# Linear attention and a gated long convolution on one core: the first batch's gate ahead of its convolution, a filter transform from half sums, v staged in pieces

## The chip, the cores and the metric

The kernel runs on 1 core of one Trainium2 chip. The metric is device time in microseconds of one execution. The engines are TensorE (PE: matmuls, with its weight loads shown as PEld), VectorE (DVE), ScalarE (ACT), GpSimd (POOL) and SyncE (SP); transfers are issued from the queues of POOL (inputs) and SP (outputs).

## The reference, cut to what matters

```python
# q, k, v: (8, 8, 576, 64); w_proj: (512, 1536); filter_fft: (576, 512); w_out: (512, 512)
def _attn_ref(q, k, v):
    theta = pi / 2 * arange(S) / S
    phi = lambda x: concat([relu(x) * cos(theta), relu(x) * sin(theta)], -1)   # 64 -> 128
    kv = einsum('bhsf,bhsd->bhfd', phi(k), v)
    z = sum(phi(k), axis=2)
    return einsum('bhsf,bhfd->bhsd', phi(q), kv) / (einsum('bhsf,bhf->bhs', phi(q), z) + 1e-6)

def reference(q, k, v, w_proj, filter_fft, w_out):
    x = heads side by side of _attn_ref(q, k, v)           # (8, 576, 512)
    x1, x2, x3 = split(x @ w_proj, 3)
    x2_conv = irfft(rfft(x2, axis=1) * rfft(filter_fft, axis=0), axis=1)
    return (x1 * x2_conv * x3) @ w_out
```

## The kernel before

The eight batches go one after another; all tiles of a batch fit on the chip. The names used below, for a batch b:

- `phi` (`emit_phi`): the features of q and k, 12 products each on DVE (recorded at line 90), from a raw tile that a POOL transfer fills. The raw tiles (q, k and v of all batches) share four buffers, so a load waits until an earlier raw tile was read to its end.
- `va` (`emit_va`, L114): ACT copies v of all 8 heads from its raw tile to `va`, next to a constant column.
- `qt` (L416): 48 transposes of q's features on PE, evicted by DVE (L422) and ACT (L426). `kv` (L403): 48 matmuls, evicted by ACT (L408). `num` (L440): 40 matmuls in four parts, and the division on DVE (L448), which gives `att`.
- `fx` (L463, L475): the first, fixed part of the transform over the sequence (`fm`), by four channel groups, evicted by ACT (L467, L479).
- `x2` (L498): the middle third of w_proj in three blocks of 8 matmuls of 512 columns, evicted by ACT (L503). `dft` (L512): two matmuls for each of three blocks, with the tables `tre` and `tim`, an eviction by ACT (L514) and four DVE products with the filter's transform (L517 to L522), which give `yf`.
- `gate` (L535): x1 and x3, the outer thirds of w_proj, 16 matmuls of 288 columns for each of four channel groups; ACT evicts x1 (L541) and DVE multiplies the two (L543) into `g`.
- `inv` (L561): 24 matmuls with the inverse tables `ire` and `iim`, an eviction by ACT (L565) and three DVE products (L566 to L568), the last with `g`. `out` (L584): 20 matmuls of 512 columns with w_out, evicted by ACT (L588) and stored from SP's queue.

Ahead of the loop stands a setup: the features, kv, num, fx and x2 of batch 0, the tables of the forward transform, the filter's transform (`emit_h_tables`, `emit_h`), the inverse tables (`emit_inv_tables`, whose range reduction runs on POOL, L238 and L241), and q, k and v of batch 1. The filter's transform multiplies all 576 rows of the filter (6 on each of 96 partitions) with cosines and sines: 36 matmuls of 512 columns and 6 for one extra frequency. The loop then runs, for b, dft, gate and inv of batch b, x2 of b, num and fx of b + 1, out of b - 1, and loads, features, qt and kv of b + 2. PSUM holds four units of two banks; every step above takes one or two.

Each engine executes its own instructions strictly in one order, POOL's transfers included. This order isn't the one of the calls: a scheduler lays it out when the program is built. It takes the calls' order as priority, and moves an instruction ahead where by its own reckoning of durations that one could start earlier. A wait that it reckoned shorter than it is on the chip holds up everything behind it on that engine.

The pool `late` (g, eo, y, os) takes the memory of the setup's tiles, so its first tile waits until the setup is through.

Of the kernel before, what the change touches and what calls it, by code (L numbers as in the profile page):

```python
# [17 lines left out]
def kernel(  # L18
# [320 lines left out]
    def emit_h_tables():  # L339
        frow, sj = cc["frow"], cc["sj"]  # L340
# [3 lines left out]
        hc = cc["hc"] = setupp.tile([NP, NJ, HS], FP16, tag="hc", name="hc")  # L344
        hs_ = cc["hs"] = setupp.tile([NP, NJ, HS], FP16, tag="hs_", name="hs_")
        for g in range(2):
            tn = setupp.tile([NP, NCOL], FP32, tag="tn_big", name=f"tn_h{g}")
            for jj in range(3):
                tsc(
                    tn[:, ds(jj * HS, HS)], frf, sj[0:NP, 3 * g + jj : 3 * g + jj + 1],  # L350
                    AL.mult, 1.0 / S, AL.mult,
                )
            trig(
                NP, tn,
                hs_[:, 3 * g : 3 * g + 3].rearrange("p a b -> p (a b)"),
                hc[:, 3 * g : 3 * g + 3].rearrange("p a b -> p (a b)"),
                NCOL,
            )
# [347 lines left out]
```

## Time and profile before

| | |
|---|---|
| runs | 305.18, 305.05, 301.96 us |
| median | 305.05 us |
| profiled execution | 306.0 us, of which the span from first to last instruction is 304.2 us |
| PE busy | 257.1 us, 85% of the span |
| DVE busy | 213.3 us, 70% |
| ACT busy | 199.8 us, 66% |
| POOL busy | 38.4 us, 13% |
| mean granted clock of PE | 0.948 |

All rows are of the profiled execution. Times in them are microseconds from the span's start, unless they are marked as ns. A busy share is the time that instructions of the engine were running; matmuls and weight loads overlap.

### The profile page before, as it was taken

The page shows a single profiled execution, that of the slowest core. Times are in us where ns is not written, and L with a number is a line of the kernel's source. Part 1 is how long each engine was busy: PE and PEld are TensorE (multiplying, and loading weights), DVE is VectorE, ACT ScalarE, POOL GpSimd, SP SyncE. Part 2 cuts the span into 40 slices and gives each one's busy share as a digit, 9 for nine tenths or more (in the row PEclk, how much of TensorE's full clock was granted, in tenths as well). Part 3 has the DMA queues.
Part 4 walks back from the last instruction along what each step waited for, and adds up shares of the span by engine and source line. Part 5 has one row for each costly group of instructions (what it writes and reads, how often), then busy time and mean ns, then how long its engine had stood idle before and what let it go on. Part 6 is the DMA issues. An engine that isn't in the chain of part 4 may idle for free.

```text
span 304.2 us, 6038 instructions
## 1 busy us (share of the span) xinstructions
PE 257.1 (85%) x2394; PEld 182.1 (60%) x2394; DVE 213.3 (70%) x684; ACT 199.8 (66%) x248; POOL 38.4 (13%) x43
## 2 busy tenths in 40 slices
PE   0647984589984599999999999999999999999970
PEld 0445541567862386768676866686678768757630
DVE  4999980487997285898589759966876558607900
ACT  2358672975750877977797778777487748757532
POOL 8330890110140300030012000000000000000000
PEclk9999998558999599999999999999999999999997
DMA  7999919924145590597149414003200410050055
GB/s 101 210 206 202 181 13 198 164 27 69 13 70 78 76 158 18 141 129 105 41 117 174 62 44 115 1 1 86 74 0 2 131 27 2 0 155 3 0 156 155
DMA packets 26828, 26.66 MB, mean 88 GB/s; under 512 B 1616, under 2 KB 22096, under 8 KB 26800
## 3 DMA queue, kind: packets, MB, share of 16 engines
q0 software_dynamic: 21040, 16.84, 37.0%
q1 hardware_dynamic: 5760, 9.44, 11.3%
q8 instruction: 18, 0.29, 0.4%
q14 instruction: 10, 0.08, 0.1%
HBM read 33.69 MB, written 9.44 MB: 142 GB/s over the span
## 4 chain that ended last, share of the span: by engine, by line
PE 59%; DVE 17%; DMA 9%; ACT 5%; POOL 3%; issue 3%; SPq 1%; ACTq 0%; POOLq 0%; DVEq 0%
PE x L535 21%; PE out L584 9%; PE inv L561 7%; DMA vraw<-in_v_dram 7%; PE x L498 6%; PE qt L416 6%; DVE kp L90 5%; PE fx L463 4%; POOL tg_a L238 3%; DVE qp L90 3%; DVE att L448 3%; PE dft L512 2%; ACT x2f L503 2%; DMA qraw<-in_q_dram 2%; PE kv L403 2%
## 5 line engine op out<-in xcount | busy, mean ns | idle before, releaser
L535 PE MATMUL x<-fx,wp 128*128 128x288 f16 x512 | 69.7, 292 | 0.0
L535 PEld LDWEIGHTS <-wp 128*128 128x128 f16 x512 | 51.1, 100 | 15.0 <-issue 1.0
L498 PE MATMUL x<-wp,fx 128*96 128x512 f16 x192 | 46.6, 391 | 2.8 <-ACT fx L479 1.5
L467 ACT CAST fx<-fx 128x960 f16<-128x960 f32 x32 | 30.3, 958 | 15.2 <-PE fx L463 15.2
L416 PE MATMUL qt<-perm,qp 96*128 96x96 f16 x384 | 23.6, 222 | 17.0 <-DVE qp L90 8.6
L584 PE MATMUL out<-wo,y 128*128 128x512 f16 x160 | 37.4, 379 | 0.0
L503 ACT ACTIVATE x2f<-x 96x1024 f16<-96x1024 f32 x24 | 24.1, 1017 | 18.2 <-PE x L498 18.2
L416 PEld LDWEIGHTS <-qp 96*128 96x128 f16 x384 | 21.1, 106 | 22.2 <-DVE qp L90 9.9
L498 PEld LDWEIGHTS <-fx 128*96 128x96 f16 x192 | 22.8, 127 | 18.9 <-DVE att L448 2.0
L543 DVE TENSOR_TENSOR g<-x,x1s 128x288 f16<-128x288 f32 x64 | 27.1, 444 | 8.1 <-PE x L535 8.1
L114 ACT COPY va<-vraw 96x3072 f16<-96x3072 f16 x8 | 22.0, 2754 | 16.0 <-DMA vraw<-in_v_dram 16.0
L588 ACT ACTIVATE os<-out 128x1024 f32<-128x1024 f32 (+1 forms) x24 | 20.7, 882 | 15.5 <-PE out L584 10.9
L517 DVE TENSOR_TENSOR m<-xf,ha 96x1024 f16<-96x1024 f16 x24 | 16.3, 679 | 19.9 <-ACT xf L514 19.8
L426 ACT COPY qpt<-qt 128x600 f16<-128x600 f16 x32 | 20.0, 661 | 13.9 <-DVE qpt L422 13.8
L448 DVE TENSOR_TENSOR att<-num,rcp 128x640 f16<-128x640 f32 x32 | 26.0, 819 | 0.2
L541 ACT CAST x1s<-x 128x576 f16<-128x576 f32 x32 | 20.5, 640 | 7.2 <-PE x L535 4.8
L422 DVE COPY qpt<-qt 128x600 f16<-128x600 f16 x32 | 14.7, 466 | 14.2 <-PE qt L416 13.8
L584 PEld LDWEIGHTS <-y 128*128 128x128 f16 x160 | 15.1, 98 | 15.3
L514 ACT CAST xf<-dft 96x1024 f16<-96x1024 f32 x24 | 23.5, 1009 | 0.8 <-PE dft L512 0.8
L561 PEld LDWEIGHTS <-yf 96*128 96x128 f16 x192 | 18.6, 98 | 4.4
L403 PE MATMUL kv<-va,kp 96*128 96x65 f16 x384 | 15.8, 206 | 5.5 <-ACT va L114 4.0
L463 PE MATMUL fx<-fm,att 128*128 128x240 f16 x128 | 19.6, 284 | 0.8 <-DVE att L448 0.8
(145 smaller groups left out, 396.7 us busy)
## 6 DMA issues: line engine op xcount, KB each, us to landing
qraw<-in_q_dram POOLq DMA_DIRECT2D x8, 576.0 KB, 6.2
kraw<-in_k_dram POOLq DMA_DIRECT2D x8, 576.0 KB, 7.8
vraw<-in_v_dram POOLq DMA_DIRECT2D x8, 576.0 KB, 8.5
out_dram<-os SPq DMA_DIRECT2D x24, 192.0 KB, 2.6
out_dram<-os SPq DMA_DIRECT2D x24, 128.0 KB, 2.4
wp<-in_moe_w_proj_dram POOLq DMA_DIRECT2D x3, 512.0 KB, 14.2
out_dram<-os SPq DMA_DIRECT2D x24, 64.0 KB, 2.0
filt<-in_moe_filter_fft_dram POOLq DMA_DIRECT2D x1, 576.0 KB, 10.4
```

The source lines that it names most:

```text
L90: nc.vector.tensor_scalar(out=out, in0=in0, scalar1=s1, scalar2=s2, op0=op0, op1=op1)
L416: nc.tensor.transpose(u[:, hh, ds(j * NP, NP)], qp[:, j, 2 * hp + hh].rearrange("p a b -> p (a b)"), perm,)
L448: nc.vector.tensor_tensor(out=att[:, :, ds(hp * 128, 128)].rearrange("p t (h d) -> p h t d", h=2), in0=nv[:, :, :, 0:D], in1=rcp.unsqueeze ...
L463: nc.tensor.matmul(u[:, t // 2, 0:480].rearrange("p (g o) -> p g o", o=20)[:, :, ds((t % 2) * 10, 10)], att[:, t, ds(c * 128, 128)], fm, s ...
L467: nc.scalar.copy(out=fx[:, c, :, 0:40].rearrange("p g (u o) -> p u g o", u=2), in_=u[:, :, 0:480].rearrange("p u (g o) -> p u g o", o=20),)
L498: nc.tensor.matmul(u[0:NP, comp], fx[:, c, ds(comp * 6 + 2 * bl, 2)].rearrange("p a b -> p (a b)"), wp16[:, c, ds(DM, DM)], start=(c == 0) ...
L503: nc.scalar.mul(out=x2f[:, bl], in_=u[0:NP], mul=X2SC)
L514: nc.scalar.copy(out=xf, in_=u[0:NP])
L535: nc.tensor.matmul(u[:, hf, 0:HS], wp16[:, i, ds(w * DM + c * 128, 128)], fx[:, i, ds(12 + 6 * hf, 6)].rearrange("p a b -> p (a b)"), star ...
L543: nc.vector.tensor_tensor(out=(g[:, c, 0:HS] if hf == 0 else g[:, c, HS:S][:, ::-1]).rearrange("p (j i o) -> p j i o", j=3, i=6), in0=us[1 ...
L561: nc.tensor.matmul(u[:, comp, 0:HS], yf[:, bl, comp, ds(c * 128, 128)], tab[:, bl], start=(bl == 0), stop=(bl == 2),)
L584: nc.tensor.matmul(u[:, x], y[:, c, ds(OT[t], 128)], wo16[:, c], start=(c == 0), stop=(c == NC - 1),)
```

## The change

Four things are changed.

- Order: in the setup, the gate of batch 0 goes behind its fx and ahead of the forward tables and x2. `g` moves from the pool `late` to the pool `work`, so that it doesn't wait for the setup's end. The rest of batch 0 (dft, inv) and num and fx of batch 1 are written into the setup as well, with loads, features, va, qt and kv of batch 2; the loop begins at batch 1.
- Loads: w_proj's outer thirds are first, the middle third next, then q and k of batch 1, the filter, v of batch 1 and w_out.
- Filter: it is loaded as two halves of 288 rows, 3 rows on each of 96 partitions. POOL makes the sum and the difference of the halves (`feo`, 96x1536 each). The blocks 1 and 2 of the transform take one of these each (3 matmuls instead of 6 for each part); block 0 takes both halves, the second one with tables (`hb`) multiplied by an alternating sign on DVE; the extra frequency takes 3 matmuls. The tables need one round instead of two. The tiles `ha` and `hi` become one tile `h3` (imaginary, real, real part), evicted in one instruction a block.
- `va` is copied in four pieces of two heads.

```diff
     def emit_va(b):
-        nc.scalar.copy(
-            out=va_buf[b % 2][:, :, :, 0:D],
-            in_=raw_t[(b, "v")].rearrange("p h (j d) -> p h j d", j=NJ),
-        )
+        for x in range(4):
+            hs = slice(2 * x, 2 * x + 2)
+            nc.scalar.copy(
+                out=va_buf[b % 2][:, hs, :, 0:D],
+                in_=raw_t[(b, "v")][:, hs].rearrange("p h (j d) -> p h j d", j=NJ),
+            )
...
     def load_filter():
-        nc.gpsimd.dma_start(out=filt16, in_=moe_filter_fft.rearrange("(p j) n -> p (j n)", j=NJ))
+        for x in range(2):
+            nc.gpsimd.dma_start(
+                out=filt16[:, x],
+                in_=moe_filter_fft[ds(x * HS, HS)].rearrange("(p j) n -> p (j n)", j=3),
+            )
...
-        hc = cc["hc"] = setupp.tile([NP, NJ, HS], FP16, tag="hc", name="hc")
-        hs_ = cc["hs"] = setupp.tile([NP, NJ, HS], FP16, tag="hs_", name="hs_")
-        for g in range(2):
-            tn = setupp.tile([NP, NCOL], FP32, tag="tn_big", name=f"tn_h{g}")
...
+        tn = setupp.tile([NP, NCOL], FP32, tag="tn_big", name="tn_h")
+        for j in range(3):
+            tsc(tn[:, ds(j * HS, HS)], frf, s3[0:NP, j : j + 1], AL.mult, 1.0 / S, AL.mult)
+        trig(NP, tn, hs_.rearrange("p a b -> p (a b)"), hc.rearrange("p a b -> p (a b)"), NCOL)
+
+        hb = cc["hb"] = setupp.tile([NP, 2, 3, NP], FP16, tag="hb", name="hb")
+        for x, tab in ((0, hs_), (1, hc)):
+            nc.vector.tensor_tensor(
+                out=hb[:, x], in0=tab[:, :, 0:NP],
+                in1=cc["sgn"].unsqueeze(1).to_broadcast([NP, 3, NP]), op=AL.mult,
+            )
...
     def emit_h():
+        for x, op in ((0, AL.add), (1, AL.subtract)):
+            nc.gpsimd.tensor_tensor(
+                out=feo[:, x].rearrange("p j n -> p (j n)"), in0=filt16[:, 0], in1=filt16[:, 1], op=op
+            )
         for bl in range(3):
             u = unit(f"h_ps{bl}")
-            for ci, tab in ((0, hc), (1, hs_)):
-                for j in range(NJ):
+            for ci, tab in ((0, hs_), (1, hc)):
+                if bl == 0:
+                    mm = [(tab[:, j, 0:NP], fa[:, 0, j]) for j in range(3)]
+                    mm += [(hb[:, ci, j], fa[:, 1, j]) for j in range(3)]
+                else:
+                    mm = [(tab[:, j, ds(bl * NP, NP)], feo[:, 2 - bl, j]) for j in range(3)]
+                for x, (l, r) in enumerate(mm):
                     nc.tensor.matmul(
-                        u[0:NP, ci], tab[:, j, ds(bl * NP, NP)], filt16[:, j],
-                        start=(j == 0), stop=(j == NJ - 1),
+                        u[0:NP, ci], l, r, start=(x == 0), stop=(x == len(mm) - 1)
                     )
-            nc.scalar.activation(out=ha[:, bl, 0], in_=u[0:NP, 0], func=AF.Copy, scale=sc)
-            nc.scalar.activation(out=hi[:, bl], in_=u[0:NP, 1], func=AF.Copy, scale=sc)
-            nc.vector.tensor_copy(out=ha[:, bl, 1], in_=ha[:, bl, 0])
+            nc.scalar.activation(out=h3[:, bl, 0:2], in_=u[0:NP], func=AF.Copy, scale=sc)
+            nc.vector.tensor_copy(out=h3[:, bl, 2], in_=h3[:, bl, 1])
...
     def emit_gate(b, c):
-            moe[b]["g"] = late["p"].tile([128, NC, S], FP16, tag="g", name=f"g{b}")
+            moe.setdefault(b, {})["g"] = work.tile([128, NC, S], FP16, tag="g", name=f"g{b}")
...
-    load_filter()
-    load_wp(1)
     load_wp(0)
     load_wp(2)
+    load_wp(1)
+    load_qk(1, "q")
+    load_qk(1, "k")
+    load_filter()
+    load_v(1)
+    load_wo()
     emit_cols()
     emit_pads()
+    emit_fm()
...
     emit_kv(0)
-    emit_fm()
     for hp in range(4):
         emit_num(0, hp)
     emit_fx(0)
+    emit_rows()
+    for c in range(NC):
+        emit_gate(0, c)
+    emit_fwd_tables()
     emit_x2(0)
-    emit_rows()
-    emit_fwd_tables()
-    emit_input_dma(1)
-    load_wo()
-    emit_h_tables()
-    emit_h()
-    emit_inv_tables()
     emit_phi(1, "q")
     for hp in range(4):
         emit_qt(1, hp)
+    emit_h_tables()
     emit_phi(1, "k")
     emit_va(1)
     emit_kv(1)
+    emit_h()
+    for hp in range(4):
+        emit_num(1, hp)
+    emit_dft(0)
+    emit_inv_tables()
+    emit_fx(1)
     setup_stack.close()
     late["p"] = ctx.enter_context(tc.tile_pool(name="late", bufs=1))
-
-    for b in range(0, B + 1):
+    for c in range(NC):
+        emit_inv(0, c)
+    emit_input_dma(2)
+    emit_phi(2, "q")
+    emit_phi(2, "k")
+    emit_va(2)
+    for hp in range(4):
+        emit_qt(2, hp)
+    emit_kv(2)
+
+    for b in range(1, B + 1):
```

## Rows read from the trace of the kernel before

**Rows 1.** The page's first part: busy us, share of the span, instructions, by engine.
```profile
PE 257.1 (85%) x2394; PEld 182.1 (60%) x2394; DVE 213.3 (70%) x684; ACT 199.8 (66%) x248; POOL 38.4 (13%) x43
```

**Rows 2.** Busy time by stretch; last columns granted clock, DMA share, GB/s.
```profile
30.70:82.60 51.90, 41.96 (x317) 28.64 (x318) 35.71 (x103) 34.47 (x41) 16.58 (x9) 0.80 0.64 95
48.00:56.80 8.80, 0.69 (x13) 0.58 (x13) 0.47 (x1) 3.74 (x4) 0.70 (x1) 0.66 1.31 203
56.80:65.50 8.70, 7.99 (x125) 7.82 (x125) 6.46 (x22) 6.75 (x9) 0.07 (x1) 0.50 0.56 76
94.70:102.00 7.30, 0.67 (x4) 0.28 (x3) 2.43 (x8) 3.75 (x3) 0.71 (x1) 0.77 0.12 17
133.70:163.40 29.70, 28.96 (x295) 20.94 (x295) 24.14 (x74) 23.11 (x29) 2.31 (x3) 1.00 0.60 105
```

**Rows 3.** The chain that ended last, at the holes: start, us, what.
```profile
31.68 9.09 POOL tg_a L238
...
43.66 9.38 DMA vraw<-in_v_dram
...
87.56 10.66 DMA vraw<-in_v_dram
98.25 2.75 ACT va L114
```

**Rows 4.** The waits: who waited for whom, total us, times, longest.
```profile
ACT va L114 <- DMA vraw<-in_v_dram: 16.0, 3, 7.5
```

**Rows 5.** The chain again, in the rhythm of the loop, PE's steps.
```profile
133.73 0.59 PE dft L512 x2
134.32 1.96 PE x L535 x16
...
144.13 2.94 PE inv L561 x24
147.07 1.73 PE out L584 x8
148.80 0.51 PE qt L416 x12
...
163.35 0.59 PE dft L512 x2
...
241.88 1.52 PE kv L403 x48
243.41 1.74 PE x L498 x8
245.15 0.62 PE num L440 x20
```

**Rows 6.** The timeline: start, us, engine, line, operation; idle before in brackets.
```profile
14.93 2.77 ACT L114 COPY va<-vraw 96x3072 f16<-96x3072 f16 x1
17.75 2.80 PE L403 MATMUL kv<-va,kp 96*128 96x65 f16 x48 [4.01 <-ACT va L114]
30.76 6.83 PE L498 MATMUL x<-wp,fx 128*96 128x512 f16 x24 [1.47 <-ACT fx L479]
33.23 2.75 ACT L114 COPY va<-vraw 96x3072 f16<-96x3072 f16 x1 [2.53 <-DMA vraw<-in_v_dram]
40.84 2.17 DVE L90 TENSOR_SCALAR qp<-qraw,ccol 96x512 f16<-96x512 f16 x1
40.85 2.00 POOL L241 TENSOR_TENSOR tg_a<-tg_a,tn_inv 96x864 f32<-96x864 f32 x1
```

**Rows 7.** Groups of instructions: line, engine, shape, count, busy us, mean ns.
```profile
L114 ACT COPY va<-vraw 96x3072 f16<-96x3072 f16 x8 | 22.0, 2754 | 16.0 <-DMA vraw<-in_v_dram 16.0
L248 ACT ACTIVATE tg_a<-tg_a 96x864 f32<-96x864 f32 x3 | 2.8, 920 | 0.1
...
L244 DVE SCALAR_TENSOR_TENSOR tg_a<-tg_a,tn_h 96x864 f32<-96x864 f32 x2 | 2.1, 1040 | 0.0
L224 DVE TENSOR_TENSOR fm<-coef,match 128x240 f16<-128x240 f32 x1 | 0.4, 391 | 0.0
```

More of the change, by code (lines that the diff above doesn't have):

```diff
@@ L343, in emit_h_tables @@
         nc.vector.memset(wr_col[0:1], 1.0 / S)
-        hc = cc["hc"] = setupp.tile([NP, NJ, HS], FP16, tag="hc", name="hc")
-        hs_ = cc["hs"] = setupp.tile([NP, NJ, HS], FP16, tag="hs_", name="hs_")
-        for g in range(2):
-            tn = setupp.tile([NP, NCOL], FP32, tag="tn_big", name=f"tn_h{g}")
[L348 to L357, printed above, removed]
-            )
+        s3 = small("s3", 3)
@@ new lines, in emit_h_tables @@
+        nc.vector.tensor_copy(out=s3, in_=cc["s3_i"])
+        hc = cc["hc"] = setupp.tile([NP, 3, HS], FP16, tag="hc", name="hc")
+        hs_ = cc["hs"] = setupp.tile([NP, 3, HS], FP16, tag="hs_", name="hs_")
+        tn = setupp.tile([NP, NCOL], FP32, tag="tn_big", name="tn_h")
+        for j in range(3):
+            tsc(tn[:, ds(j * HS, HS)], frf, s3[0:NP, j : j + 1], AL.mult, 1.0 / S, AL.mult)
+        trig(NP, tn, hs_.rearrange("p a b -> p (a b)"), hc.rearrange("p a b -> p (a b)"), NCOL)
@@ new lines, in emit_h_tables @@
+        hb = cc["hb"] = setupp.tile([NP, 2, 3, NP], FP16, tag="hb", name="hb")
[3 more added lines that the diff above has]
+                in1=cc["sgn"].unsqueeze(1).to_broadcast([NP, 3, NP]), op=AL.mult,
+            )
+        alt = cc["alt"] = setupp.tile([NP, 2], FP16, tag="alt", name="alt")
+        par = cc["par"]
+        tsc(alt[:, 0:1], par[0:NP], -2.0, AL.mult, 1.0, AL.add)
+        tsc(alt[:, 1:2], par[0:NP], 2.0, AL.mult, -1.0, AL.add)
@@ L376, in emit_h @@
-            nc.vector.tensor_copy(out=ha[:, bl, 1], in_=ha[:, bl, 0])
+            nc.scalar.activation(out=h3[:, bl, 0:2], in_=u[0:NP], func=AF.Copy, scale=sc)
+            nc.vector.tensor_copy(out=h3[:, bl, 2], in_=h3[:, bl, 1])
         u = unit("h_nyq")
-        for j in range(NJ):
+        for j in range(3):
             nc.tensor.matmul(
-                u[0:1, 0], alt[:, j : j + 1], filt16[:, j], start=(j == 0), stop=(j == NJ - 1)
+                u[0:1, 0], alt[:, j % 2 : j % 2 + 1], feo[:, 0, j], start=(j == 0), stop=(j == 2)
@@ L381, in emit_h @@
             )
-        nc.scalar.activation(out=ha[0:1, 0, 1], in_=u[0:1, 0], func=AF.Copy, scale=1.0 / S)
+        nc.scalar.activation(out=h3[0:1, 0, 2], in_=u[0:1, 0], func=AF.Copy, scale=1.0 / S)
     kp_t, qp_t, kvs_t, att_t, fx_t, xt_t = {}, {}, {}, {}, {}, {}
@@ L491, in emit_x2 @@
         if 0 in bls:
-            moe[b] = {"x2f": work.tile([NP, 3, 2, DM], FP16, tag="x2f", name=f"x2f{b}")}
+            moe.setdefault(b, {})["x2f"] = work.tile([NP, 3, 2, DM], FP16, tag="x2f", name=f"x2f{b}")
         x2f = moe[b]["x2f"]
```

21 lines of the change are left out of this document (10 added, 11 removed).

## The prediction, made before the result was known

> **What bounds the kernel now.** I read the page's first part, then the busy time by stretch, then the chain of waits, then the timeline around its holes. The first part [rows 1] has TensorE (PE) busy 85% of the span and no other engine above 70%. That average hides two different regimes. In the stretch table [rows 2] PE is busy nearly all the time while the loop is in its rhythm, but from 30.7 to 102 us there are two holes: 48.0 to 56.8 with 0.69 us of PE work, and 94.7 to 102.0 with 0.67. [...]
>
> The chain of waits names the cause of both holes [rows 3]: a load of v, 9.38 us in one and 10.66 us in the other, after which ScalarE (ACT) makes its copy of v into va. ACT takes its instructions in order, and the copy stands ahead of evictions whose inputs are long there: in the first hole those of the filter's transform, in the second those of x2. PE waits for these. The waits view puts the sum of three such waits at 16.0 us [rows 4]. Ahead of the first load stands 9.09 us of GpSimd (POOL) work for the inverse tables: the loads are issued from POOL's queue, so nothing is issued meanwhile.
>
> In the rhythm, PE is the bound. From one dft to the next takes 163.35 - 133.73 = 29.62 us [rows 5]. The same rows price the work at 2.4 GHz: x2 3 x 1.74 = 5.22; num 2 x 0.61 = 1.22; gate 4 x 1.96 = 7.84; inv 2.94; gate, fx and inv together 147.07 - 134.32 = 12.75, so fx 1.97; out 2.5 x 1.73 = 4.33; qt 4 x 0.51 = 2.04; kv 1.52. A matmul of 512 columns is 1.74 / 8 = 0.2175, so dft's six are 1.31. Sum 28.4; a cycle has 1.22 us beyond it.
>
> From 30.7 to 133.7 us, 103.0 us, PE does: batch 0 x2, dft, gate, inv, out 21.64; batch 1 all but out 24.07; batch 2 qt, kv, num, fx, x2 11.97; batch 3 qt, kv, num 4.78; the filter's 42 matmuls 9.1. That is 71.6, so 31.4 us are lost there. What lies behind 133.7 is untouched by the change but for va's pieces.
>
> **The change part by part.**
>
> *Order.* Batch 0's gate needs only fx and w_proj's outer thirds, which now load first; it moves to 30.7 us and fills PE while tables and filter are made. All its work comes along: 64 matmuls, 4 evictions, 8 products. By itself it saves nothing; it is cover, 7.84 us, for the holes. Batch 1's num and fx move ahead of batch 0's inverse too. In all PE has then, in the stretch of 103.0 us, 62.46 + 27 x 0.2175 = 68.3 us. I keep two losses: the slow start of PE's long work (the first x2 took 6.83 instead of 5.22 [rows 6], 1.6), which the gate will now pay, and 1.22 for each of some 2.3 cycles, 2.8. That gives 72.7, a gain of 30.3 with no hole left. This is the upper bound.
>
> *Filter transform.* 42 matmuls become 12 + 6 + 6 + 3 = 27: 3.3 us of PE, counted in the 68.3. One table round goes: three activations of about 0.92 [rows 7], 2.8 us of ACT; on VectorE (DVE) five instructions of which the largest is 1.04, so 2 to 3 us, against two products for hb at about 0.4 each (nearest row: the fm product, 0.39 [rows 7]) and two tiny ones. These hide under loads before 30.7; without that cover 1 us. Three evictions of two halves replace six of one half: the same columns. The filter comes in two transfers of the same bytes. Both at nothing: ACT stands idle beside them, and one more issue on POOL is under a microsecond.
>
> *Sum and difference on POOL.* This is new: two POOL instructions of 96x1536. The trace has two POOL rows to price them, both of 96x864 in f32 [rows 3, 6]: 2.00 us for the two-input form (2.3 ns an element) and 9.09 us for the one-input form (10.5 ns). So 7.1 us for both at the one end, 32.3 us at the other. I take the lower, since it is the same operation; but DVE ran back to back next to the 9.09 and this may be why, so I keep the upper. The other direction shows too: beside the 2.00 one DVE instruction, a product of 96x512, took 2.17 us [rows 6]. [...]
>
> *DVE in the filled stretch.* From 30.7 to the end of batch 0's inverse (82.6) DVE has 35.71 us of work now [rows 2]. PE's part of it after the change is x2, dft, gate, inv of batch 0 (17.31), qt, kv, num, fx of batch 1 (6.75), filter 5.9, slow start 1.6: 31.6 us. DVE's is then about 33, plus up to 7.1 of standing for POOL; six of it (phi of batch 2) can slip. From 0 to 9 us on the path; I take 5.
>
> *POOL's queue.* Behind these two and the inverse tables stand the loads of k and v of batch 2. Before, v of batch 2 was issued at 43.66 [rows 3]. The filter lands later than before: ten loads were issued before v of batch 1 was there, whose copy starts at 33.23 [rows 6], and the filter is now ninth, one load of 0.58 MB at 203 GB/s [rows 2] or 2.8 us earlier, so at about 30. If POOL then does 7.1 + 9.09 + 2.00, it is free at about 48.5, 5 us later than before, and v lands near 58. Batch 2's kv is due on PE near 64: in time. But an early va piece in ACT's queue can hold it as before.
>
> *va in four pieces.* An instruction of 864 elements takes 0.92 and one of 3072 takes 2.75 [rows 7]: 0.83 ns an element and 0.2 fixed, so four pieces cost some 0.3 us more a batch, less than the 6.6 us that ACT stands idle in a cycle (23.11 busy of 29.7 [rows 2]); if that cover went, 2.4 us over eight batches. A piece waits for the same single load, so splitting doesn't end a wait. It lets kv start after the first piece: batch 0's copy starts at 14.93 and kv at 17.75, for 2.80 us [rows 6]. Four pieces end near 18.0, the last quarter of kv is 0.7, so kv ends at 18.7 instead of 20.5. I take 1.5 of the 1.8, since att on DVE is behind it; from 0 to 1.8.
>
> *Waits on v.* Both holes with the half-clock stretch cost: 8.1 + 6.9 idle, and 56.8 to 65.5 took 8.7 for 4.3 us of work: 4.4. Together 19.4. The inverse tables stay on POOL and v's loads in its queue, so I don't count both as gone: I leave one of the second's size, 7.5. Bounds 0 and 19.4.
>
> Sum by the profiled execution: span 304.2 - 30.3 - 1.5 = 272.4, + 5 + 7.5 = 284.9. This execution took 306.0 by its own time and the median is 305.05; I add to the span what the median has over 304.2, 0.85: **286 us**.
>
> **The rivals.**
>
> *POOL becomes the bound.* At 10.5 ns an element the two new instructions take 32.3; from 30 with the tables' 11.1 ahead, the difference is there at 73.4. PE has until then gate, x2, qt, kv, num, fx (19.8) and 1.6 of slow start: done at 52.2. It waits 21 us, and some 3 follow at the lower clock, as behind the first hole: 272.4 + 24 = 296.4 by span, 297. For it: 9.09 us. Against it: the same form took 2.00. It decides from the point where the difference comes after 52. [...]
>
> *Both holes stay.* ACT's order puts va pieces ahead of urgent evictions again: 272.4 + 5 + 19.4 = 296.8, 298. For it: three waits of this kind now. Against: later cycles have none, and the cover is there.
>
> *No hole comes back:* 272.4 to 277, 273 to 278.
>
> *Slower.* A piece of batch 2's va stands in ACT's queue ahead of the filter's evictions, and v of batch 2 is issued only when POOL is through, at 73.4, landing 9.4 later at 82.8. Then va 3, evictions 3, num, dft, fx, inv and the products between them 9, lower clock 2: batch 0's inverse ends near 100 instead of 82.6, and without the second hole (7 + 1) the kernel is 9 us slower, 314. It decides from a landing after about 73. Against it: this needs POOL at its slowest and that order.
>
> **How the numbers follow.** Forecast 0.52 (its own range 279 to 293), no hole 0.12, POOL bound 0.14, both holes 0.12, slower mechanism 0.10, of which half gets only as far as no change. A difference of under 1% (302.0 to 308.1 us) is about what a measurement of this kernel can't tell from none. Faster 0.88, since all but the last case and a tail of 0.02 end below 302; same 0.06; slower 0.06. The range from 275 to 300 takes in the bounds of the two waits, and leaves out the lowest of "no hole" and the slower case, under 0.2.
>
> **What would show it.** In the changed kernel's timeline: gate's matmuls at about 30 us, at double spacing first; 27 filter matmuls; two POOL instructions of 3 to 4 us each (over 10 is the first rival); PE's holes between 30 and 100 summing to about 15 instead of 31; batch 0's inverse ending near 70; the rhythm still 29.6 us. I am wrong if va waits for v as long as before, if the rhythm itself changes by half a us, or if DVE stands for POOL for more than 9 us.

## The result and the profile after

| | before | after |
|---|---|---|
| median of the runs shown | 305.05 us | 295.81 us (295.68 to 295.97) |
| measured side by side | 304.31 us | 295.81 us, ratio 0.973, 95% interval 0.967 to 0.979 |
| span of the profiled execution | 304.2 us | 294.2 us |

The change makes the kernel 2.7% faster. The forecast was 286 us, a gain of 6%; the time lies inside its range, but the gain is less than half of the one forecast. All ratios below are to the kernel before, measured beside it on the same chip, with 95% intervals in brackets. In the changed kernel the line numbers move: va is L116, x2 L515 with its eviction L520, the gate L552 with the evictions L558, num L457, dft L529 with L531, fx L480 with L484, inv L578; the sum and difference `feo` L376, the range reduction of the inverse tables L245 and L248. A kernel that adds lines has its own numbers. The kernel before had medians from 302.56 to 305.24 us in the five measurements, so of kernels from different measurements the times are compared as well as the ratios.

The page's first part (busy us, share, instructions) and the chain of waits of the changed kernel:

```profile
PE 255.1 (87%) x2379; PEld 179.8 (61%) x2379; DVE 211.0 (72%) x678; ACT 198.5 (67%) x266; POOL 40.2 (14%) x47
...
17.97 15.28 DMA vraw<-in_v_dram
33.27 1.57 ACT va L116 x2
45.65 6.16 POOL tg_a L245
...
61.49 6.13 DMA vraw<-in_v_dram
...
93.72 0.59 PE dft L529 x2
...
123.35 0.59 PE dft L529 x2
```

The loop's rhythm is untouched: 123.35 - 93.72 = 29.63 us for a cycle, as in [rows 5]. The dft of batch 2 (here and below its last block, the one that the chain lists) starts at 123.35 instead of 133.73, and these 10.4 us are all of the gain, which is 10.0 us by the spans. They lie ahead of the rhythm, where loads of v and POOL's table pass still stand in the chain, as in [rows 3].

The changed kernel by stretch, cut where one of PE's steps ends (busy us and instruction counts of PE, PEld, DVE, ACT, POOL; then granted clock, DMA share, GB/s):

```profile
28.70:40.60 11.90, 10.02 (x65) 6.87 (x65) 7.67 (x22) 6.54 (x10) 9.06 (x5) 0.86 0.75 114
40.60:45.80 5.20, 5.20 (x26) 2.94 (x25) 5.20 (x18) 2.38 (x3) 0.98 (x2) 1.00 1.31 204
45.80:55.10 9.30, 3.19 (x50) 2.95 (x49) 5.45 (x16) 5.11 (x8) 8.77 (x3) 0.68 0.78 121
55.10:66.30 11.20, 11.20 (x80) 6.66 (x78) 7.43 (x27) 8.07 (x12) 2.10 (x4) 0.66 0.71 98
66.30:81.10 14.80, 11.21 (x91) 6.82 (x91) 11.92 (x32) 12.64 (x17) 1.15 (x2) 0.84 0.72 99
81.10:93.70 12.60, 12.27 (x165) 9.30 (x164) 12.27 (x43) 9.36 (x14) 1.62 (x2) 0.91 0.34 49
93.70:123.30 29.60, 28.88 (x294) 20.96 (x294) 24.55 (x75) 23.27 (x32) 2.32 (x3) 1.00 0.61 106
```

Against the prediction's prices for PE's work, which sum to 68.3 us, each stretch shows what is lost (the exact starts of the steps are 28.68, 40.58, 45.75, 55.08, 66.25, 81.13, 93.72 and 123.35):

| stretch | PE's steps in it | takes | work | lost |
|---|---|---|---|---|
| 28.7 to 40.6 | gate of batch 0 | 11.9 | 7.8 | 4.1 |
| 40.6 to 45.8 | x2 of batch 0 | 5.2 | 5.2 | 0 |
| 45.8 to 55.1 | qt of batch 1 | 9.3 | 2.0 | 7.3 |
| 55.1 to 66.3 | kv of batch 1, filter's transform | 11.2 | 7.4 | 3.8 |
| 66.3 to 81.1 | num of 1, dft of 0, fx of 1, inv of 0 | 14.9 | 7.4 | 7.4 |
| 81.1 to 93.7 | qt, kv, num of 2, x2 of 1 | 12.6 | 10.0 | 2.6 |
| 93.7 to 123.4 | one cycle | 29.6 | 28.4 | 1.2 |

Of the 2.6 us in the last row but one, 0.9 are four dft matmuls of batch 1, which the prices have in the cycle alone. In all 26.4 us are lost, where 31.4 were lost before and the forecast kept 16.9 (1.6 + 2.8 + 5 + 7.5). The timeline of the changed kernel at the holes, engine by engine (start, us, engine, line, operation; idle before in brackets):

```profile
33.27 1.57 ACT L116 COPY va<-vraw 96x768 f16<-96x768 f16 x2 [4.65 <-DMA vraw<-in_v_dram]
34.75 0.63 ACT L558 CAST x1s<-x 128x576 f16<-128x576 f32 x1
...
42.50 1.02 ACT L520 ACTIVATE x2f<-x 96x1024 f16<-96x1024 f32 x1 [0.54 <-PE x L515]
49.99 0.83 ACT L116 COPY va<-vraw 96x768 f16<-96x768 f16 x1 [6.47 <-DMA vraw<-in_v_dram]
50.73 1.01 ACT L520 ACTIVATE x2f<-x 96x1024 f16<-96x1024 f32 x1
...
35.42 3.14 PE L552 MATMUL x<-fx,wp 128*128 128x288 f16 x24 [1.03 <-ACT x1s L558]
...
51.79 1.12 PE L433 MATMUL qt<-perm,qp 96*128 96x96 f16 x12 [4.85 <-ACT x2f L520]
...
30.42 6.75 POOL L376 TENSOR_TENSOR feo<-filt 96x1536 f16<-96x1536 f16 x2 [10.88 <-DMA filt<-in_moe_filter_fft_dram]
...
38.71 0.77 POOL L111 DMA_DIRECT2D vraw<-in_v_dram  x1
```

ACT stands 4.65 us for v of batch 1 ahead of the gate's first eviction, and 6.47 us for v of batch 2 ahead of x2's second. In the first case PE has filled its four PSUM units at 34.4 and waits 1.03 us for the eviction of x1; in the second x2's blocks were there before 46, and PE waits 4.85 us. The sum of ACT's waits for v is about what it was in [rows 4]:

```profile
ACT va L116 <- DMA vraw<-in_v_dram: 16.9, 4, 6.5
```

So the change took two holes apart and got two back, ahead of other evictions. What follows asks whether that alone is the missing 10 us, and which part of the change carries the gain that is there.

### The profile page after: what moved, and what is told of

It is laid out like the page before. It is cut to its first block, busy times and chain, and to the rows that moved or that the text cites. A ratio compares the mean times of both kernels' runs of the same rounds, so it can differ in the third digit from the quotient of the medians.

```text
span 294.2 us, 6029 instructions
## 1 busy us (share of the span) xinstructions
PE 255.1 (87%) x2379; PEld 179.8 (61%) x2379; DVE 211.0 (72%) x678; ACT 198.5 (67%) x266; POOL 40.2 (14%) x47
## 4 chain that ended last, share of the span: by engine, by line
PE 55%; DVE 17%; DMA 10%; ACT 7%; issue 4%; POOL 3%; SPq 1%; ACTq 0%; POOLq 0%; DVEq 0%
PE x L552 19%; PE out L601 9%; PE inv L578 9%; DMA vraw<-in_v_dram 7%; PE x L515 7%; DVE kp L90 7%; PE qt L433 5%; PE fx L480 3%; DVE qp L90 3%; DVE att L465 3%; ACT x2f L520 2%; POOL tg_a L245 2%; DMA qraw<-in_q_dram 2%; PE dft L529 1%; ACT va L116 1%
## 5 line engine op out<-in xcount | busy, mean ns | idle before, releaser
L552 PE MATMUL x<-fx,wp 128*128 128x288 f16 x512 | 69.0, 290 | 3.1 <-ACT fx L496 1.5
L552 PEld LDWEIGHTS <-wp 128*128 128x128 f16 x512 | 50.6, 99 | 17.7 <-issue 2.9
L515 PE MATMUL x<-wp,fx 128*96 128x512 f16 x192 | 45.1, 381 | 2.1 <-DVE att L465 1.7
L484 ACT CAST fx<-fx 128x960 f16<-128x960 f32 x32 | 30.3, 960 | 14.7 <-PE fx L480 14.6
L433 PE MATMUL qt<-perm,qp 96*128 96x96 f16 x384 | 24.2, 224 | 16.0 <-DVE qp L90 9.8
L520 ACT ACTIVATE x2f<-x 96x1024 f16<-96x1024 f32 x24 | 24.5, 1022 | 19.4 <-PE x L515 19.4
L116 ACT COPY va<-vraw 96x768 f16<-96x768 f16 x32 | 26.0, 836 | 16.9 <-DMA vraw<-in_v_dram 16.9
L433 PEld LDWEIGHTS <-qp 96*128 96x128 f16 x384 | 21.8, 108 | 21.2 <-DVE qp L90 10.9
L515 PEld LDWEIGHTS <-fx 128*96 128x96 f16 x192 | 22.2, 123 | 17.2 <-DVE att L465 2.5
L439 DVE COPY qpt<-qt 128x600 f16<-128x600 f16 x32 | 14.8, 467 | 17.0 <-PE qt L433 16.5
L534 DVE TENSOR_TENSOR m<-xf,h 96x1024 f16<-96x1024 f16 x24 | 16.4, 682 | 13.4 <-ACT xf L531 13.2
L578 PEld LDWEIGHTS <-yf 96*128 96x128 f16 x192 | 19.3, 102 | 7.9 <-DVE yf L538 1.5
L531 ACT CAST xf<-dft 96x1024 f16<-96x1024 f32 x24 | 23.4, 1008 | 0.0
L558 ACT CAST x1s<-x 128x576 f16<-128x576 f32 x32 | 20.4, 639 | 3.9 <-PE x L552 1.7
L582 ACT CAST eo<-inv 128x576 f16<-128x576 f32 x32 | 19.3, 657 | 3.1 <-PE inv L578 2.8
L480 PE MATMUL fx<-fm,att 128*128 128x240 f16 x128 | 18.9, 274 | 1.1 <-ACT fx L484 0.6
```

What stands on the lines that cost most here:

```text
L116: nc.scalar.copy(out=va_buf[b % 2][:, hs, :, 0:D], in_=raw_t[(b, "v")][:, hs].rearrange("p h (j d) -> p h j d", j=NJ),)
L433: nc.tensor.transpose(u[:, hh, ds(j * NP, NP)], qp[:, j, 2 * hp + hh].rearrange("p a b -> p (a b)"), perm,)
L480: nc.tensor.matmul(u[:, t // 2, 0:480].rearrange("p (g o) -> p g o", o=20)[:, :, ds((t % 2) * 10, 10)], att[:, t, ds(c * 128, 128)], fm, s ...
L484: nc.scalar.copy(out=fx[:, c, :, 0:40].rearrange("p g (u o) -> p u g o", u=2), in_=u[:, :, 0:480].rearrange("p u (g o) -> p u g o", o=20),)
L515: nc.tensor.matmul(u[0:NP, comp], fx[:, c, ds(comp * 6 + 2 * bl, 2)].rearrange("p a b -> p (a b)"), wp16[:, c, ds(DM, DM)], start=(c == 0) ...
L520: nc.scalar.mul(out=x2f[:, bl], in_=u[0:NP], mul=X2SC)
```

## Experiments: the waits

**The copies of v moved back (e1), the sum and difference moved to DVE (e2), both (e7).** Theory: the va pieces that wait for v ahead of urgent evictions are the loss. Rival: POOL's new work is.

In e1 each batch's pieces stand in ACT's order behind a named eviction:

```diff
+    VA_BEHIND = {1: 'x1s(0,3)', 2: 'kvs(1)', 3: 'fxc(1)'}
...
+        with tc.issue_after(mark[VA_BEHIND[b]].ins):
+            emit_va_(b)
```

In e2 DVE makes `feo`:

```diff
-            nc.gpsimd.tensor_tensor(
+            nc.vector.tensor_tensor(
                 out=feo[:, x].rearrange("p j n -> p (j n)"), in0=filt16[:, 0], in1=filt16[:, 1], op=op
```

> The changed kernel, with va of batch 1 ordered behind batch 0's last gate eviction on ACT, va of batch 2 behind batch 1's kv eviction, va of batch 3 behind batch 1's last fx eviction; nothing waits longer for data than before. Theory (va pieces stand in ACT's order ahead of evictions and wait for v): the holes of PE at 31 to 35 and 46 to 52 us go, with the lower clock behind them; 284 to 290 us. Rival (the stretch to 123 us is bound by DVE's and ACT's work, and the wait only hides it): 294 to 296 us.

> The changed kernel, with the sum and the difference of the filter's halves on DVE in place of POOL. Theory that POOL's queue makes v of batch 2 late (its two instructions wait for the filter until 30.4 and hold the loads behind them until 37.1): q and k of batch 2 are issued before 31 us, v of batch 2 lands at 43 to 45 in place of 50, and the second hole shrinks: 288 to 292 us. Theory that only ACT's order matters, whatever the landing: 294 to 297 us, the DVE's work of 2 us added.

> The changed kernel with both edits of the first round together: va of batches 1, 2, 3 ordered behind evictions, and the sum and difference on DVE. Either one alone gave nothing. Theory (several waits stand side by side before the same evictions, so one is worth nothing while the next is there; left here is only POOL's range reduction of the inverse tables, some 3 us): 288 to 292 us. Rival (from 30 to 95 us ACT and DVE are the bound, whatever waits): 294 to 297 us.

| kernel | median us | ratio |
|---|---|---|
| e1 | 294.93 | 0.973 [0.969, 0.977] |
| e2 | 296.43 | 0.977 [0.973, 0.981] |
| e7 | 292.79 | 0.967 [0.961, 0.974] |

Neither alone moves the time: e1 and e2 landed in the ranges of their rivals, e7 0.8 us above the range of its theory. The timelines show why. In e1 (ACT, DVE, POOL, then PE) va is out of the way, and the gate waits all the same:

```profile
38.51 0.92 ACT L263 ACTIVATE hs__666<-tg_a 96x864 f16<-96x864 f32 x1 [6.08 <-DVE tg_a L260]
...
30.18 3.19 DVE L90 TENSOR_SCALAR kp<-kraw,ccol 96x512 f16<-96x512 f16 x1
33.30 3.48 DVE L259 TENSOR_SCALAR tg_a<-tn_h 96x864 f32<-96x864 f32 x1
36.70 0.81 DVE L569 TENSOR_TENSOR g<-x,x1s 128x288 f16<-128x288 f32 x2
37.43 1.04 DVE L260 SCALAR_TENSOR_TENSOR tg_a<-tg_a,tn_h 96x864 f32<-96x864 f32 x1
...
30.14 6.17 POOL L385 TENSOR_TENSOR feo<-filt 96x1536 f16<-96x1536 f16 x2 [11.18 <-DMA filt<-in_moe_filter_fft_dram]
...
37.56 5.73 PE L561 MATMUL x<-fx,wp 128*128 128x288 f16 x24 [3.85 <-DVE g L569]
```

PE's wait of 3.85 us ends with DVE's products `g` of the gate. Ahead of these, in DVE's order, stand a product for the features and a pass over the filter's tables, which took 3.19 and 3.48 us while POOL made `feo`. In e7, which differs from e1 only in that DVE makes `feo`, such products take 0.34 to 0.62 us and the pass 0.59. The tables' `hs`, which stands ahead of the gate's third eviction in ACT's order, waits for the same pass. In the changed kernel the wait for v, a few us ahead of the same tables, had hidden it: there `hs` starts at 38.12 and waits 0.75. In e2 it is the other way round: DVE is free, and ACT waits for v as in the changed kernel:

```profile
33.08 1.56 ACT L116 COPY va<-vraw 96x768 f16<-96x768 f16 x2 [4.87 <-DMA vraw<-in_v_dram]
...
44.37 1.56 ACT L116 COPY va<-vraw 96x768 f16<-96x768 f16 x2 [3.45 <-DMA vraw<-in_v_dram]
...
65.95 0.83 ACT L116 COPY va<-vraw 96x768 f16<-96x768 f16 x1 [5.39 <-DMA vraw<-in_v_dram]
```

With both gone (e7) a third wait stands in ACT's order, for POOL's inverse tables, again ahead of the evictions that PE wants:

```profile
54.75 0.92 ACT L263 ACTIVATE iim<-tg_a 96x864 f16<-96x864 f32 x1 [6.53 <-POOL tg_a L257]
...
47.43 7.29 POOL L257 TENSOR_TENSOR tg_a<-tg_a,tn_inv 96x864 f32<-96x864 f32 x1
```

**All three gone (e8), and each put back.** e8 is e7 with the range reduction of the inverse tables on DVE, and with two batches' copies of v placed where v is there (batch 2 behind the filter's last eviction, batch 4 behind the last x2 of batch 1). e15 is e8 with the inverse tables back on POOL; e16 is e8 with `feo` back on POOL; e9 has both on DVE, but leaves the copies of v where the scheduler puts them.

Against e7, e8 has both of these edits; e16 has both, with `feo` back on POOL, e15 the first alone, and e9 the second alone, without any `VA_BEHIND`:

```diff
-    VA_BEHIND = {1: 'x1s(0,3)', 2: 'kvs(1)', 3: 'fxc(1)'}
+    VA_BEHIND = {1: 'x1s(0,3)', 2: 'nyq', 3: 'fxc(1)', 4: 'x2f(1,2)'}
...
-        trig(NP, tn, iim.rearrange("p a b -> p (a b)"), ire.rearrange("p a b -> p (a b)"), NCOL, True)
+        trig(NP, tn, iim.rearrange("p a b -> p (a b)"), ire.rearrange("p a b -> p (a b)"), NCOL)
```

> As the run before, with the inverse tables' range reduction on DVE too, so that POOL only issues loads, and va of batch 2 behind the filter's last eviction, va of batch 4 behind batch 1's last x2 eviction. Theory of waits side by side: no wait for v or POOL is left ahead of an eviction, 282 to 288 us. Rival (ACT and DVE are the bound): 292 to 296 us.

> The changed kernel with sum, difference and the inverse tables' range reduction on DVE, va in the order that the scheduler chooses. Theory of waits side by side: the wait for v of batch 1 holds the gate until 33 us as in the changed kernel, those behind it shrink: 290 to 294 us. If POOL's work is all that matters: as low as the run before, 282 to 288.

> e8_no_wait_left with the range reduction of the inverse tables back on POOL. It differs from e7_va_behind_feo_dve only in where the second and fourth batch's copies of v stand. If POOL's tables are the wait that e7 had left: ratio 0.962 to 0.970, with iim waiting some 6 us for POOL. If the place of the copies was: 0.943 to 0.950.

> e8_no_wait_left with the sum and difference of the filter halves back on POOL. If they cost by themselves (DVE's table pass stands for them and hs waits some 6 us ahead of the gate's evictions, as in e1_va_behind): ratio 0.957 to 0.970. If that wait only counted beside the others: 0.943 to 0.950.

| kernel | what still waits | median us | ratio | dft of batch 2 starts |
|---|---|---|---|---|
| e8 | none of the three | 286.53 | 0.946 [0.941, 0.951] | 114.43 |
| e15 | POOL's inverse tables | 290.07 | 0.958 [0.953, 0.962] | 117.48 |
| e16 | POOL's sum and difference | 290.58 | 0.957 [0.951, 0.964] | 118.82 |
| e9 | the copies of v | 293.53 | 0.970 [0.966, 0.975] | 121.50 |

e8 is 3% faster than the changed kernel and takes the 286 us that were forecast for that one, though by another sum, as shown below. e8 and e9 landed in the first of their ranges. e8's stretches at the same steps, and its dft of batch 2:

```profile
28.70:36.60 7.90, 7.89 (x65) 6.33 (x65) 7.90 (x24) 4.77 (x7) 0.77 (x1) 1.00 1.28 204
36.60:47.60 11.00, 9.34 (x121) 6.98 (x120) 11.00 (x31) 9.63 (x14) 1.54 (x2) 0.95 1.17 171
...
47.60:52.70 5.10, 5.10 (x16) 2.46 (x14) 3.83 (x15) 2.13 (x4) 2.71 (x1) 0.50 0.07 8
...
56.40:68.20 11.80, 7.54 (x76) 4.54 (x76) 11.77 (x34) 11.75 (x16) 1.02 (x2) 0.95 0.73 102
68.20:72.00 3.80, 3.80 (x17) 2.38 (x18) 1.73 (x7) 3.10 (x5) 0.63 (x1) 0.50 0.67 82
...
114.43 0.59 PE dft L538 x2
```

The gate takes 7.9 us for 7.8 of work. DVE is now busy all the time up to 47.6 and for 11.77 of the 11.8 us from 56.4 on, and the chain that ended last runs through DVE from 23.3 to 44.0 and from 55.5 to 68.1. So e8's rival named an engine that does bind once the waits are gone, at a time more than 5 us too long.

e15 landed between its two expectations and e16 at the lower end of one: a wait put back costs 1.2 points, not nothing, and not the 2 points that 6.5 us would be. In e15 ACT waits 6.54 us for POOL's table pass, and the dft of batch 2 comes 3.1 us later than in e8; in e16 the wait for DVE's table pass is shorter than in e1, and a second one follows (3.80 us, where e8 has 1.13), together 6.6 us, and the dft comes 4.4 us later. ACT in e15, then ACT and DVE in e16:

```profile
53.70 0.92 ACT L263 ACTIVATE iim<-tg_a 96x864 f16<-96x864 f32 x1 [6.54 <-POOL tg_a L257]
```

```profile
34.85 0.92 ACT L263 ACTIVATE hs__666<-tg_a 96x864 f16<-96x864 f32 x1 [2.84 <-DVE tg_a L260]
...
47.25 0.92 ACT L263 ACTIVATE iim<-tg_a 96x864 f16<-96x864 f32 x1 [3.80 <-DVE tg_a L260]
...
31.46 3.36 DVE L260 SCALAR_TENSOR_TENSOR tg_a<-tg_a,tn_h 96x864 f32<-96x864 f32 x1
```

The copies of v cost the most when they are all that waits: e9 against e8, 2.4 points or 7.0 us. And e15 against e7, which differ in the place of two batches' copies alone, is 1.0 point apart at intervals that overlap a little; in the two traces the gate's 64 matmuls take 9.53 us in e7, at the lower clock first (0.57 to 0.62 from 28.7 to 32.7, as the last section has it), and 8.00 in e15, so the place of the copies needn't be all of it. The three costs, 2.4, 1.2 and 1.2, sum to 4.8 points, and yet only 2.8 lie between the changed kernel and e8, while e1 and e2, which take one away first, gain nothing: the waits hide each other.

## Experiments: the parts of the change

**With the waits as they come.** e4 is the change with the old filter transform, e3 the change with v in one piece, e14 the change's order alone, that of the loads with it (both taken back). e6 and e5 are the kernel before with one part added, the pieces or the new transform.

The edit of e3 takes back the first hunk of the change's diff, that of e4 the hunks of `load_filter`, the tables and `emit_h`, e14 has both; e6 and e5 make the same hunks on the kernel before:

```diff
     def emit_va(b):
-        for x in range(4):
-            hs = slice(2 * x, 2 * x + 2)
-            nc.scalar.copy(
-                out=va_buf[b % 2][:, hs, :, 0:D],
...
+        nc.scalar.copy(
+            out=va_buf[b % 2][:, :, :, 0:D],
```

```diff
     def emit_h():
-        for x, op in ((0, AL.add), (1, AL.subtract)):
-            nc.gpsimd.tensor_tensor(
...
-            for ci, tab in ((0, hs_), (1, hc)):
+            for ci, tab in ((0, hc), (1, hs_)):
+                for j in range(NJ):
```

> The changed kernel, with va in one copy again. If the pieces helped (evictions slip between them, kv starts after the first): 297 to 300 us. If the pieces cost (0.3 us more ACT work a batch, and more places in ACT's order where a wait for v stands): 291 to 294 us.

> The changed kernel, with the filter loaded and transformed as in the kernel before (42 matmuls, two table rounds, nothing of it on POOL). If the filter's transform gives what its matmuls and tables count (3.3 us of PE, 2.8 of ACT, 2.5 of DVE): 298 to 302 us. If POOL's two instructions take it back by holding the loads: 293 to 296 us.

> The kernel before, with the new filter transform alone (27 matmuls, one table round, sum and difference on POOL). If a wait for v behind POOL's queue sets the time there: v of batch 2 comes 6 us later or is not moved, and the kernel gains nothing or loses up to 2%: 302 to 309 us against 303 to 305 of before. If the transform's work counts: 3 to 6 us faster, 298 to 301 us.

> The kernel before, with va in four pieces and nothing else. If a piece waits as the whole copy does: 302 to 305 us, as before. If evictions slip between the pieces, or kv starts earlier: 298 to 301.

> The change's order alone: old filter transform, v in one piece, the waits as the scheduler puts them. If the order alone carries what the change brought: ratio 0.970 to 0.985 (v in one piece cost 0.7% in e3_va_whole). If the order brings nothing while the waits stand and the pieces brought it all: 0.99 to 1.01.

| kernel | parts in it | median us | ratio |
|---|---|---|---|
| e14 | order | 299.03 | 0.987 [0.981, 0.993] |
| e6 | pieces | 299.66 | 0.985 [0.978, 0.991] |
| e4 | order, pieces | 295.82 | 0.976 [0.971, 0.981] |
| e3 | order, transform | 297.46 | 0.980 [0.976, 0.984] |
| e5 | transform | 309.81 | 1.021 [1.014, 1.028] |
| the change | all | 295.81 | 0.973 [0.967, 0.979] |

The order alone brings 1.3%, the pieces alone 1.5%, both together 2.4%; the transform adds nothing that can be told to these, and alone it makes the kernel 2.1% slower. e3, e4 and e6 each landed in one of their two ranges; e5 is 0.8 us above the upper end of its first, and e14 lies just above its first range and below its second.

Part of both gains is the start, not a wait taken away: PE's long work begins at 27.36 in e6 and 28.66 in e14, against 30.76 before. The prediction gave the pieces 1.5 us at the start and no other effect. In e6 the first copies still wait, but a piece can stand between two evictions where the whole copy held both. The hole of [rows 2] is moved by this, not filled. Here is its stretch in e6, then ACT's order and PE before it:

```profile
48.00:56.80 8.80, 7.97 (x60) 4.92 (x59) 1.40 (x5) 6.21 (x11) 0.77 (x1) 0.85 1.31 203
```

```profile
33.02 0.83 ACT L116 COPY va<-vraw 96x768 f16<-96x768 f16 x1 [5.71 <-DMA vraw<-in_v_dram]
33.75 0.92 ACT L249 ACTIVATE hs__499<-tg_a 96x864 f16<-96x864 f32 x1
34.58 1.00 ACT L505 ACTIVATE x2f<-x 96x1024 f16<-96x1024 f32 x1
...
36.30 0.82 ACT L116 COPY va<-vraw 96x768 f16<-96x768 f16 x1
...
38.99 4.07 PE L371 MATMUL h_ps<-filt,hc 96*96 96x512 f16 x9 [6.25 <-ACT hc L251]
```

PE works 7.97 us in that stretch, against 0.69, but before it PE stands 6.25 us for ACT's tables, which come behind the wait for v. At kv of batch 1 e6 is 2.2 us ahead of the kernel before (57.50 against 59.68), less than its lead at the start, and at the dft of batch 2 it is 6.2 us ahead (127.57 against 133.73): in between, the copy behind the second hole waits 3.68 us instead of 7.51. POOL's first pass over the inverse tables lies elsewhere too (39.03, 3.23 us), so what the pieces do by themselves is not separated from what the scheduler laid out anew.

What made e5 slower begins at 18.25, where POOL makes `feo`: a DVE instruction on 128x1 takes 7.05 us from 17.36 (0.15 in the kernel before; the chain that ended last has it with 6.96), and ACT waits 8.99 us for the table pass behind it. The tables for the inverse then come 6 us later than in the kernel before, with POOL's first pass over them at 36.68 (31.68 in [rows 3]). e5 with `feo` on DVE was not run. ACT and POOL in e5:

```profile
26.89 0.44 ACT L252 ACTIVATE tim<-tg_a 96x288 f16<-96x288 f32 x1 [8.99 <-DVE tg_a L249]
...
49.19 0.92 ACT L252 ACTIVATE iim<-tg_a 96x864 f16<-96x864 f32 x1 [7.10 <-POOL tg_a L246]
...
18.25 6.13 POOL L374 TENSOR_TENSOR feo<-filt 96x1536 f16<-96x1536 f16 x2
...
36.68 9.63 POOL L243 TENSOR_SCALAR tg_a<-tn_inv 96x864 f32<-96x864 f32 x1 [12.29 <-DVE tn_inv L90]
```

**With no wait left.** e11 is e8 with the old transform, e12 is e8 with v in one piece, e13 with both taken back; e10 is the kernel before with the same two edits against waits (inverse tables on DVE, the copies of batches 2 and 4 behind the same evictions; those of batches 1 and 3, which e8 also places, stay where the scheduler puts them).

> The changed kernel without waits (286.5 us), with the old filter transform. If the transform's 15 matmuls and second table round are on the path once nothing waits: 289 to 292 us. If they are hidden even then: 286 to 288.

> The changed kernel without waits (286.5 us), with va in one copy. If the pieces only mattered where a wait stood: 286 to 287 us, at most 1 us from kv's later start in batch 0. If splitting helps by itself: 288 to 290.

> The change's order (the first batch's gate ahead of its convolution) with the old filter transform and v copied in one piece, and with no copy of v and no table pass of POOL left ahead of an eviction. If the order is worth its cover only where nothing waits, and the other two parts are worth nothing then, this has the time of e8_no_wait_left: ratio 0.942 to 0.948. If the filter transform or the pieces carry something that only shows when both are taken back: 0.955 or more.

> The kernel before, none of the change in it, with the waits taken away in the same way: va of batch 2 behind the filter's last eviction, va of batch 4 behind batch 1's last x2 eviction, the inverse tables' range reduction on DVE. If the two holes are what the kernel before loses (19 us with the lower clock) and the gate's new place is only cover: 284 to 289 us, level with the changed kernel without waits (286.5). If the gate ahead and the lighter filter give something of their own: 290 to 296.

| kernel | parts in it | median us | ratio |
|---|---|---|---|
| e8 | order, pieces, transform | 286.53 | 0.946 [0.941, 0.951] |
| e11 | order, pieces | 287.38 | 0.944 [0.938, 0.951] |
| e12 | order, transform | 286.61 | 0.942 [0.935, 0.950] |
| e13 | order | 287.67 | 0.950 [0.945, 0.954] |
| e10 | none | 297.94 | 0.978 [0.973, 0.984] |

The ratios of the first four can't be told apart: without waits the pieces and the transform are worth little or nothing, and the order carries the gain. e13's four runs (287.2 to 288.7 us) do lie above e8's (285.5 to 286.7), from another measurement, so up to 0.4% may be in the two parts together. e11 and e12 landed in their ranges for parts that are hidden, e13 between its two. e10, at 297.94 us, lies above both of its ranges. Between e10 and the four lie about 3 points, an upper bound for the worth of the order, since e10 isn't wholly free of waits; its copy for batch 3 stands ahead of an eviction for 6 us (ACT in e10):

```profile
63.72 2.75 ACT L116 COPY va<-vraw 96x3072 f16<-96x3072 f16 x1 [6.00 <-DMA vraw<-in_v_dram]
```

Why 15 matmuls fewer bring nothing against e13 can be read from the clock. In e13 the old transform's 42 matmuls run in 9.4 us at a granted clock of 1.00, and the 10.5 us before them have 1.00 as well; in e8 the new one's 27 take 8.8 us, the first 12 of them at 0.50 (from 47.6 to 52.7). The two stretches, of e13 and of e8:

```profile
46.50:55.90 9.40, 9.38 (x45) 4.59 (x43) 9.12 (x34) 7.59 (x12) 3.69 (x3) 1.00 0.86 123
```

```profile
47.60:56.40 8.80, 8.80 (x31) 4.11 (x28) 6.03 (x23) 4.88 (x7) 3.48 (x2) 0.68 0.49 69
```

In the 10.5 us ahead of its transform PE was busy 8.84 us in e8 (2.24 of the 3.9 from 41.7 to 45.6) and 9.60 in e13. In e11, with the old transform too, PE was busy 9.64 of 11.0 us up to 47, and the granted clock was 0.70 from 47 to 58: against e11 the clock is not the reason, and the 0.9 us between the two medians lies within e11's own runs (285.9 to 289.0). Why the clock fell in two and not in the third was not settled.

## Why the prediction was right or wrong

The mechanism of the holes was right, and so were the rhythm and POOL's price. The start came out by luck: fx is through 2.0 us earlier (1.5 forecast, from the pieces), but the gate starts as early with v in one piece (28.66 in e14, 28.48 in e3, 28.68 in the changed kernel), so in the changed kernel the order brings it. The size was wrong, and the step that failed is the account of what is lost, 16.9 us: its largest term, **the waits on v**, 7.5 us, "one of the second's size", with the gate as cover, and beside it 9.4 us for everything else. By the table of stretches:

| term of the sum | forecast | lost at its place, after |
|---|---|---|
| slow start of PE's long work, paid by the gate | 1.6 | 1.6 (clock 0.58 from 28.7 to 32.7: 20 matmuls in 4.0 us, for 2.45 of work) |
| waits on v, with the half-clock stretch behind | 7.5 | 13.6 (the gate's other 2.5, 7.3, 3.8) |
| DVE, and its standing for POOL | 5 | 7.4, from num to inv, with the chain on ACT |
| PE's cycles beyond their work | 2.8 | 3.8 |
| sum | 16.9 | 26.4 |

The right column goes by place. e8 divides it by cause: without the three waits it still loses 17.4 us over the same steps, none in the gate and x2, 1.8 at qt, 3.4 at kv and the filter's transform, 8.1 from num to inv, 2.6 and 1.5 behind. So about 9.0 of the 26.4 us go with all three waits together, where the sum had 7.5 for v alone, and 17.4 stay where the sum had 9.4. Most of the 9.5 us by which the sum fell short is thus in steps that PE does not run at their price even when nothing waits for a load: in e8 DVE has no time left at qt and hardly any from num on, and the filter's transform starts at a granted clock of 0.50. This division is an estimate, since e8 also moves some 3.5 us of POOL's work to DVE (1.82, 0.59 and 1.04). For PE's prices the prediction names 2.4 GHz, a frequency that no run shows; what the rows show is steps at a granted clock of 1.00, with 0.2175 us for a matmul of 512 columns.

- *Waits on v.* The prediction's own sign of being wrong came true: va waits 16.9 us for v, as long as before (16.0). The prediction let the gate cover the wait, and did not ask where in ACT's order the first copy would stand against the gate's own evictions. v of batch 1 landed at 33.2, as in [rows 6]; what moved was PE, which now had x1 for ACT to evict ahead of that and its four units full at 34.4. PE's own idle time in the gate is 1.9 us, 1.03 of it for x1's eviction behind v; 0.57 is for `g` on DVE. So the moved work got the hole that it was to fill. Of batch 2's v the prediction had said that an early piece could hold the queue, and one did: but ahead of x2, not of kv, from 43.5 and not up to 58, because its load is issued ahead of the inverse tables (38.71) and not behind them. The half-clock stretch came back behind it, 55.1 to 62.8 at a granted clock of 0.50.
- *Both holes stay* was the nearest rival by its mechanism, and by its time (298 us) as near as POOL as the bound (297; POOL's two instructions took 6.75 us, not 32.3). It had 0.12. Its 19.4 holds a slip: 7.30 - 0.67 of [rows 2] is 6.6, not 6.9.
- *One term as an independent cost.* The deeper mistake is to price the waits as terms that add up. Three waits stood side by side: for v and for POOL's inverse tables in ACT's order, and for POOL's `feo` in DVE's. Taking one away uncovers the next (e1, e2); with all gone the time is the forecast's (e8: from the first step to the dft of batch 2 it takes 114.43 - 28.71 = 85.7 us; the forecast's sum is 72.7 + 12.5 = 85.2). That agreement is luck, one of the sum and not of its terms: e8 has no wait on v there, and loses 17.4 us elsewhere.
- *DVE and its standing for POOL.* The prediction took 5 us for DVE's work and its standing for POOL. In the changed kernel the largest case costs little: a table pass of 1.94 us instead of 1.04 [rows 7]. The stretch from 66.3 to 81.1 loses 7.4 for another reason: PE's steps there (num, dft, fx, inv) wait for the evictions and products of the ones before, ACT and DVE are busy 12.64 and 11.92 of 14.8 us, the chain runs through ACT's evictions with pieces of va between them, and the inverse runs at clock 0.50. In e8, with nothing but transfers on POOL, the same steps take 15.6 us, as the two rows from 56.4 to 72.0 show, with DVE busy for 11.77 of the first 11.8: the term had the right engine, but its own work binds and not POOL. The inverse of batch 0 so ended at 81.1 (near 70 expected), and at 72.0 in e8.
- *Sum and difference on POOL.* 6.75 us for both, 7.1 taken; the upper bound of 32.3 was off. The one-input row of 9.09 was no price for it: that table pass itself took from 3.12 us (e2) to 9.63 (e5). That DVE's work beside it makes the difference was not tried by itself.
- *Filter transform.* The sum counted 3.3 us of PE's work as saved and everything else about it as nothing. The saving doesn't show, with the waits (the change 295.81, e4 295.82) or without them (e8 286.53, e11 287.38). What was not seen is that alone it costs 2.1% (e5).
- *Pieces at 1.5 us* was right in size, and not for its reason: e3, with v in one piece, is 1.7 us slower than the changed kernel and starts no later. Alone on the kernel before they bring more (e6, as much as the order). The 0.3 us that four copies cost on ACT doesn't follow from 0.2 fixed for each, which makes 0.6, but is what e8 shows: four in a row take 3.03 us, one took 2.75.

What stays open: why e8's clock fell ahead of the filter's transform and e13's did not; and whether the chain of num, dft, fx and inv, 8 us of loss even in e8, can be filled by an order that puts PE's qt of batch 2 between, with DVE as busy there as it is. Neither was tried.

## What to carry to other kernels

When work is moved to fill a hole, its own evictions join the queue that made the hole: look at what stands in that engine's order between the moved work's first result and its eviction, and when that lands, before counting the work as cover. Waits ahead of the same steps need not add up, so an experiment that takes one away and sees nothing says nothing about the others; take all away first, then put each back (here 2.4, 1.2 and 1.2 points, against none seen one by one). The fastest versions here (e8, and with it e11 and e12, 286.5 to 287.4 us) need no new arithmetic: e8 is the change with the copies of v placed where their load has landed, and with POOL's passes on DVE.

## What the runs showed of the hardware

- Some of DVE's instructions took several times as long beside POOL's work, and POOL's own passes of one form took over three times as long in one kernel as in another. In e1, beside POOL's `feo`, DVE's one-input pass over 96x864 took 3.48 us and a product of 96x512 took 3.19; in e7, with `feo` on DVE, they took 0.59 and 0.34 to 0.62. DVE's two-input pass took 3.36 (e16), 1.94 (after) and 1.04 (e7). In e5 an instruction on 128x1 took 7.05 us beside `feo`, and 0.15 in the kernel before. POOL's two-input pass took 7.29 us in e7 beside back-to-back DVE products of f16 and 2.01 in the changed kernel, its one-input pass between 3.12 and 9.63. The prediction had both directions as bounds; that one instruction's duration would vary this much with what runs beside it was not expected. What decides which of the instructions takes longer was not settled: in e1 the product of 3.19 us starts 0.04 us behind `feo`, and in the changed kernel the one-input pass starts 0.15 us behind `feo` (30.42) and takes 0.60; the profile's spans on POOL are rough.
- The two filter products on DVE took 1.81 us (e15, at 39.03) for what POOL needed 6.75 for. The move of `feo` to DVE costs DVE about a quarter of that time, and it is not free: in e8 the chain that ended last has `feo` on DVE with 1.73 us.
- The granted clock was at 0.50 from 55.1 to 62.8 in the changed kernel, behind 9.3 us in which PE was busy 3.19, and again from 76.8 to 81.1, behind 10.5 us in which it was busy 6.97: both times the step behind PE's waits ran at half the clock.
- The slow start of the gate, a sure 1.6 us in the sum, is not in every kernel: from 28.7 to 32.7 the granted clock was 0.57 to 0.62 in the traces of the changed kernel, e4, e7 and e14, and 1.00 in the ten others that have the gate ahead. In all of them PE was busy 5.6 to 6.3 us from 20.0 to 28.6; what decides it stays open.
